# Fewer, larger logits batches, one more FP32 sum on VectorE, and down sums run ahead, in an attention + GLU kernel

## The chip, the cores and the metric

The kernel runs on one core of one Trainium2 chip. The metric is device microseconds of one execution. The granted TensorE clock was 1.000 in profiled runs. TensorE is called PE below, its weight loads PEld, VectorE DVE, ScalarE ACT.

## The reference, cut to what matters

```python
# x: [1, 2048, 640]; H = 32 heads of Dh = 20; window of W = 8 keys, 2 apart
xn = layernorm(x)
q, k, v = split(xn @ wqkv)                            # per head
logits[s, w] = q[s] . k[s - 2 w] / sqrt(Dh)           # -1e9 where s - 2w < 0
attn = softmax(logits over w)
o[s] = sum_w attn[s, w] * v[s - 2 w]
out = x + o @ wo + ((xn @ w_gate) * (xn @ w_up)) @ w_down     # F = 1536
```

## The kernel before

This kernel doesn't compute attention as matrix products of q and k on PE. DVE makes the elementwise products, and PE adds them up by multiplying with small 0/1 matrices in its 32-column tiling mode (four 128x32 tiles side by side). All other work of PE (projections, gate and up, down and output) uses the whole 128x128 array and serves as filler. PE's sums go to PSUM, a memory that the program divides into eight banks of 512 columns; "ACT evicts" means that ACT copies a bank out, after which it can be used again. A planner written in Python decides, while the program is built, where each visit to the 32-column mode goes in PE's fixed instruction order; it does so with a running estimate of PE's and DVE's time (`t_pe`, `t_dve`).

The 40 products of q and k go through a ring of buffers and are added up in batches:

```python
def qk_logits(batch):                                  # batch: list of (w, c, slot)
    for w, c, s in batch:
        for j in range(NJ):                            # four 32-column tiles, one per 512 tokens
            ... matmul(PS[32*j:32*j+32, lb], G[:, c, :], prd(s)[:, j*JB:(j+1)*JB],
                       start=(c == 0), stop=(c == NCH-1), tile_position=(0, 32*j))
    ... ACT evicts the logits of every w that is now complete

for i, (w, c) in enumerate(order):                     # 40 products
    t_dve[0] = ... + 1.14
    qk_prod(w, c, i % NPW)                             # DVE, ring of NPW = 11
    batch.append((w, c, i % NPW))
    if ready is not None and len(batch) == 2:
        run_fill(ready[1])                             # PE filler up to the time estimated
        qk_logits(ready[0]); ready = None
    if i % 20 in (7, 15, 19):                          # batches of 8, 8, 4, 8, 8, 4
        ready = (batch, t_dve[0] + 0.2); batch = []
```

The value side has 20 units (4 token blocks of 512 x 5 channel groups). A "plain" unit is one DVE pass, whose two halves PE adds up with eight matmuls. Any other unit is three DVE passes: two products in FP32 and their sum. PE then needs four matmuls.

```python
PLAIN = {0: PA, 1: PB, 2: PC, 3: PV, 4: PC, 19: PA}
GROUPS = ((0, 1, 2), (3, 4), tuple(range(5, 10)), tuple(range(10, 15)), tuple(range(15, 20)))
# pv_sum(us): PE sums of one group, one PSUM bank per unit, then ACT evicts each into OT

def tail(t, nb):                                       # output, 128 tokens x 320 columns
    b = bank()
    for i in range(NF + NCH):                          # 12 down matmuls, then 5 of the output projection
        l, x = (HT[...], WD[:, i, cols]) if i < NF else (OT[...], WO[:, i - NF, cols])
        ... matmul(PS[:, b], l, x, start=(i == 0), stop=(i == n - 1))
    ... DVE adds the residual; store
```

## Time and profile before

Three runs gave a median of 272.38 us (271.96 to 272.39). The span of the profiled run is 270.3 us.

| what | before |
|---|---|
| PE busy | 266.5 us, 99% |
| DVE busy | 224.5 us, 83% |
| ACT busy | 117.1 us, 43% |
| PE's share of the chain that ended last | 93% |

The first two lines are from the profile's page. Each engine has its busy us, share of the span and number of instructions.

```profile
span 270.3 us, 4471 instructions
PE 266.5 (99%) x1837; PEld 149.4 (55%) x1837; DVE 224.5 (83%) x276; ACT 117.1 (43%) x213; POOL 2.5 (1%) x18
```

"PE busy" alone is weak evidence. The Trainium skill, "Perfetto Trace Analysis", section "Tensor Engine Instruction (MATMUL, LD_WEIGHTS)", says that the profiler estimates the end of a matmul. This trace fits that, without proving it: a 128x512 matmul is given as 379 ns, yet the next starts about 216 ns after it (95 of them take 20.50 us below), so the durations given overlap. What ends last is told better by the chain, the work followed back from the last instruction. Its columns are start us, duration us, what (in the first line L443, projections of 256 columns). L424 are projections, L473 logits, L588 the sums of the value side, L648 down and output matmuls.

```profile
19.61 10.92 PE PS L443 x100
30.53 20.50 PE PS L424 x95
51.03 1.84 PE PS L473 x32
52.87 7.66 PE PS L424 x35
60.53 1.84 PE PS L473 x32
62.37 2.26 PE PS L424 x10
64.64 0.98 PE PS L473 x16
...
73.28 1.84 PE PS L473 x32
...
82.78 1.84 PE PS L473 x32
...
86.88 0.98 PE PS L473 x16
...
238.63 1.41 PE PS L588 x24
240.04 27.87 PE PS L648 x221
267.91 0.02 issue
```

Each line of the chain starts where the one before it ends (lines left out are marked by dots): from 15.25 us on, the chain is PE without a break. A wait shorter than the overlap, 379 - 216 = 163 ns, would not show as a break, so the starts of the single matmuls count too (in the packed trace each has its own record): after 19.61 us, two 128x512 matmuls in the 128x128 mode start 0.215 to 0.227 us apart and two 128x320 ones 0.135 to 0.147 us; longer steps (0.229 to 0.312 us) come at changes of the tiling mode alone. So PE doesn't wait, and the lengths of the lines tell what a visit to the 32-column mode costs. 32 logits matmuls take 1.84 us and 16 take 0.98 us, so four take (1.84 - 0.98) / 4 = 0.215 us and a visit has 0.12 us on top of its work. The projections behind it (35 in 7.66 us) are also 0.1 us longer than at PE's pace.

### The profile page before, as it was taken

The page shows a single profiled execution, that of the slowest core. Times are in us where ns is not written, and L with a number is a line of the kernel's source. Part 1 is how long each engine was busy: PE and PEld are TensorE (multiplying, and loading weights), DVE is VectorE, ACT ScalarE, POOL GpSimd, SP SyncE. Part 2 cuts the span into 40 slices and gives each one's busy share as a digit, 9 for nine tenths or more (in the row PEclk, how much of TensorE's full clock was granted, in tenths as well). Part 3 has the DMA queues.
Part 4 walks back from the last instruction along what each step waited for, and adds up shares of the span by engine and source line. Part 5 has one row for each costly group of instructions (what it writes and reads, how often), then busy time and mean ns, then how long its engine had stood idle before and what let it go on. Part 6 is the DMA issues. An engine that isn't in the chain of part 4 may idle for free.

```text
span 270.3 us, 4471 instructions
## 1 busy us (share of the span) xinstructions
PE 266.5 (99%) x1837; PEld 149.4 (55%) x1837; DVE 224.5 (83%) x276; ACT 117.1 (43%) x213; POOL 2.5 (1%) x18
## 2 busy tenths in 40 slices
PE   8999999999999999999999999999999999999996
PEld 3998644444443444444467744446764444767775
DVE  5899719999996799899998999999999999922212
ACT  3665666355555684666530037551007555030000
POOL 2000000000000000000000000000000000000000
DMA  6998699018989597679324341232421000021301
GB/s 205 316 134 152 103 300 402 25 57 343 387 346 406 178 358 263 182 173 338 125 82 127 94 147 66 78 81 79 142 84 49 0 2 0 27 72 49 96 29 49
DMA packets 35668, 41.53 MB, mean 154 GB/s; under 512 B 10304, under 2 KB 31808, under 8 KB 35648
## 3 DMA queue, kind: packets, MB, share of 16 engines
q1 hardware_dynamic: 35344, 40.96, 49.0%
q10 hardware_dynamic: 304, 0.30, 0.4%
q8 instruction: 14, 0.23, 0.3%
q14 instruction: 6, 0.05, 0.1%
HBM read 25.07 MB, written 13.16 MB: 141 GB/s over the span
## 4 chain that ended last, share of the span: by engine, by line
PE 93%; SPq 2%; DMA 1%; DVE 1%; issue 0%; ACT 0%
PE PS L617 39%; PE PS L648 27%; PE PS L424 16%; PE PS L443 4%; PE PS L473 3%; PE PS L588 2%; SPq L288 2%; PE PS L436 2%; DMA XST<-in_A_x_dram 1%; DVE XNS L378 0%; DVE STATS L356 0%; DVE STATS L362 0%; DVE MV L368 0%; DVE FOUT L652 0%; ACT SD L369 0%
## 5 line engine op out<-in xcount | busy, mean ns | idle before, releaser
L617 PE MATMUL PS<-XNT,WG 128*128 128x512 bf16 x240 | 59.7, 379 | 0.0
L617 PE MATMUL PS<-XNT,WU 128*128 128x512 bf16 x240 | 59.6, 379 | 0.0
L648 PE MATMUL PS<-WD,HT 128*128 128x320 bf16 (+1 forms) x396 | 57.6, 295 | 0.0
L619 ACT ACTIVATE HT<-PS 128x512 bf16<-128x512 f32 x48 | 28.8, 599 | 58.8 <-PE PS L617 57.0
L648 PEld LDWEIGHTS PS<-WD,HT 128*128 128x128 bf16 x396 | 38.1, 98 | 15.0 <-issue 0.4
L424 PE MATMUL PS<-XNT,WQKV 128*128 128x512 bf16 x200 | 44.0, 379 | 0.0
L617 PEld LDWEIGHTS PS<-XNT,WU 128*128 128x128 bf16 x240 | 23.4, 98 | 28.5 <-issue 0.4
L617 PEld LDWEIGHTS PS<-XNT,WG 128*128 128x128 bf16 x240 | 23.1, 98 | 28.9 <-ACT OT L594 0.8
L619 ACT ACTIVATE USX<-PS 128x512 bf16<-128x512 f32 x48 | 28.8, 600 | 20.1 <-PE PS L617 20.1
L652 DVE TENSOR_TENSOR FOUT<-PS,XR 128x320 bf16<-128x320 f32 (+1 forms) x33 | 15.7, 477 | 25.6 <-PE PS L648 25.5
L465 DVE TENSOR_TENSOR PRA<-QT,KT 128x2048 bf16<-128x2048 bf16 x24 | 27.6, 1218 | 7.3 <-ACT KT L429 7.3
L424 PEld LDWEIGHTS PS<-XNT,WQKV 128*128 128x128 bf16 x200 | 19.2, 98 | 24.2 <-issue 1.3
L565 DVE TENSOR_TENSOR TB<-VX,ATX 128x2048 f32<-128x2048 bf16 x14 | 31.9, 2282 | 0.0
L565 DVE TENSOR_TENSOR TA<-VX,ATX 128x2048 f32<-128x2048 bf16 x14 | 31.9, 2282 | 0.0
L648 PE MATMUL PS<-WO,OT 128*128 128x320 bf16 (+1 forms) x165 | 27.1, 295 | 0.0
L648 PEld LDWEIGHTS PS<-WO,OT 128*128 128x128 bf16 x165 | 15.9, 98 | 5.9
L622 DVE TENSOR_TENSOR HT<-HT,USX 128x512 bf16<-128x512 bf16 x48 | 19.0, 416 | 0.0
L465 DVE TENSOR_TENSOR PRB<-QT,KT 128x2048 bf16<-128x2048 bf16 x16 | 18.5, 1218 | 0.0
L429 ACT ACTIVATE VST<-PS 128x512 bf16<-128x512 f32 x20 | 12.0, 599 | 11.6 <-PE PS L424 11.6
L594 ACT ACTIVATE OT<-PS 128x512 bf16<-128x512 f32 x20 | 10.3, 609 | 9.0 <-PE PS L588 9.0
L574 DVE TENSOR_TENSOR SV<-TA,TB 128x2048 bf16<-128x2048 f32 x6 | 13.7, 2283 | 0.0
L436 PE MATMUL PS<-XNT,WQKV 128*128 128x128 bf16 x200 | 12.3, 219 | 0.4 <-ACT KT L451 0.3
(72 smaller groups left out, 190.4 us busy)
## 6 DMA issues: line engine op xcount, KB each, us to landing
VX<-v_scratch SPq DMA_DIRECT2D x20, 520.0 KB, 4.8
v_scratch<-VST SPq DMA_DIRECT2D x5, 515.5 KB, 6.5
v_scratch<-VST SPq DMA_DIRECT2D x5, 515.0 KB, 6.2
v_scratch<-VST SPq DMA_DIRECT2D x5, 514.5 KB, 5.3
v_scratch<-VST SPq DMA_DIRECT2D x5, 514.0 KB, 4.2
XR<-in_A_x_dram SPq DMA_DIRECT2D x16, 160.0 KB, 2.5
XST<-in_A_x_dram SPq DMA_DIRECT2D x15, 160.0 KB, 4.0
out_dram<-FOUT SPq DMA_DIRECT2D x15, 160.0 KB, 1.8
```

Of the source, the lines that this page charges most:

```text
L424: op("pe", (lambda l, x, c: lambda e: e.matmul(PS[:, b, :], l, x, start=(c == 0), stop=(c == NCH - 1)))(l, x, c), r=[l, x], w=[PS[:, b, :] ...
L429: op("act", lambda e: e.activation(o, PS[:, b, :], ACT.Copy), r=[PS[:, b, :]], w=[o], name=f"pev{which}_{m}_{j}")
L436: op("pe", (lambda o, l, x, st, sp: lambda e: e.matmul(o, l, x, start=st, stop=sp))(o, l, x, st, sp), r=[l, x], w=[o], name=f"pp{which}_{m ...
L443: op("pe", (lambda l, x, c: lambda e: e.matmul(o, l, x, start=(c == 0), stop=(c == NCH - 1)))(l, x, c), r=[l, x], w=[o], name=f"pw{which}_ ...
L465: op("dve", lambda e: e.tensor_tensor(prd(s), QT[:, c, :], k, ALU.mult), r=[QT[:, c, :], k], w=[prd(s)], name=f"prod{w}_{c}")
L565: op("dve", lambda e: e.tensor_tensor(t[:], vw, a, ALU.mult), r=[v, at[:, r, :], ("tsum", 0)], w=[t[:]], name=f"pv{u}_{r}")
L574: op("dve", lambda e: e.tensor_tensor(s[:], TA[:], TB[:], ALU.add), r=[TA[:], TB[:]], w=[s[:], ("tsum", 0)], name=f"pa{u}")
L617: op("pe", (lambda l, x, c: lambda e: e.matmul(PS[:, b, :], l, x, start=(c == 0), stop=(c == NCH - 1)))(l, x, c), r=[l, x], w=[PS[:, b, :] ...
L619: op("act", lambda e: e.activation(o, PS[:, b, :], ACT.Copy), r=[PS[:, b, :]], w=[o], name=f"guev{which}_{m}_{j}")
L622: h_pending.append(lambda: op("dve", lambda e: e.tensor_tensor(h, h, o, ALU.mult), r=[h, o], w=[h], name=f"h{m}_{j}"))
L648: op("pe", (lambda l, x, i, b: lambda e: e.matmul(PS[:, b, 0:wid], l, x, start=(i == 0), stop=(i == n - 1)))(l, x, i, b), r=[l, x], w=[PS[ ...
L652: op("dve", (lambda o, xr, b: lambda e: e.tensor_tensor(o, PS[:, b, 0:wid], xr, ALU.add))(o, xr, b), r=[PS[:, b, :], xr], w=[o], name=f"fi ...
```

## The change

Its intent: fill the 32-column mode better (10 products a visit, 4 visits for 6), with a larger ring so that DVE needn't wait; let DVE do the final sum of unit 19 too; and start the last token block's output groups with their down matmuls, which don't need attention, in three banks that stay open. One softmax maximum is split, so that most of it can run before the last logit. The core of the diff, with cuts marked:

```diff
-    NPA, NPW = 6, 11
+    NPA, NPB, NPW = 6, 5, 13
+    PRC = sb("PRC", [128, S], at=a_ra + 20 * JB * 2)          # and PRE: two more ring slots
...
-    PLAIN = {0: PA, 1: PB, 2: PC, 3: PV, 4: PC, 19: PA}
+    PLAIN = {0: PA, 1: PB, 2: PC, 3: PV, 4: PC}
...
-                (0.67, tt(M1, L[:, 0:4], L[:, 4:8], ALU.max, "smax1")),
+                (0.4, tt(M1[:, 3:4], L[:, 3:4], L[:, 7:8], ALU.max, "smax1")),
+            early = (0.55, tt(M1[:, 0:3], L[:, 0:3], L[:, 4:7], ALU.max, "smax0"))
...
-    def tail(t, nb):
+    def tail(t, nb, span=(0, NF + NCH)):
-            b = bank()
+            b = held_banks.pop((t, nb)) if span[0] else bank()
-            for i in range(n):
+            for i in range(*span):
+            if span[1] < n:
+                held_banks[t, nb] = b
+                return
...
-    LATE = 1.2
+    LATE = (1.2, 1.2, 2.5, 2.5, 1.2)
-    add_dn(3)
+    add_dn(3, 3)            # first the down matmuls of three groups, later their output matmuls
...
-        if i % 20 in (7, 15, 19):
-            ready = (batch, t_dve[0] + 0.2)
+        if i % 20 in (9, 19):
+            ready = (batch, t_dve[0] - 0.6)
```

`LATE` is how long after DVE's estimated end the planner puts a group's sums into PE's order.

More of the change, by code (lines that the diff above doesn't have):

```diff
@@ L232, in build_kernel @@
     a_pr = place[0]
-    NPA, NPW = 6, 11
+    NPA, NPB, NPW = 6, 5, 13
     PRA = sb("PRA", [128, NPA, S])
-    PRB = sb("PRB", [128, NPW - NPA, S], at=a_wd)
+    PRB = sb("PRB", [128, NPB, S], at=a_wd)
+    PRC = sb("PRC", [128, S], at=a_ra + 20 * JB * 2)
     def prd(s):
-        return PRA[:, s, :] if s < NPA else PRB[:, s - NPA, :]
+        if s < NPA + NPB:
+            return PRA[:, s, :] if s < NPA else PRB[:, s - NPA, :]
+        return PRC[:] if s == NPA + NPB else PRE[:]
     a_pc = a_qk + 8 * 4 * VW * 2
@@ L279, in build_kernel @@
     G = sb("G", [128, NCH, H])
+    PRE = sb("PRE", [128, S])
     PS = nc.alloc_psum_tensor("PS", [128, 8, 512], FP32)
@@ L518, in half @@
             ]
-            return head, rest
-        (h0, r0), (h1, r1) = half(0), half(1)
-        return h0 + h1 + r0 + r1
+            early = (0.55, tt(M1[:, 0:3], L[:, 0:3], L[:, 4:7], ALU.max, "smax0"))
+            return early, head, rest
+        (e0, h0, r0), (e1, h1, r1) = half(0), half(1)
+        return [e0, e1] + h0 + h1 + r0 + r1
     def attn_move(j):
@@ L630, in build_kernel @@
     stores = []
-    def tail(t, nb):
+    held_banks = {}
+    def tail(t, nb, span=(0, NF + NCH)):
         j, rows = t // 4, slice((t % 4) * TS, (t % 4 + 1) * TS)
@@ L767, in build_kernel, with add_dn @@
     units_done = [0]
-    def add_dn(j):
-        for st in range(4):
-            for nb in range(2):
-                fill.append(("dn", j, lambda st=st, nb=nb: tail(4 * j + st, nb)))
+    def add_dn(j, ahead=0):
+        groups = [(4 * j + st, nb) for st in range(4) for nb in range(2)]
+        for t, nb in groups[:ahead]:
+            fill.append((1.63, lambda t=t, nb=nb: tail(t, nb, (0, NF))))
+        for i, (t, nb) in enumerate(groups):
+            span = (NF if i < ahead else 0, NF + NCH)
+            fill.append(("dn", j, 0.136 * (span[1] - span[0]), lambda t=t, nb=nb, span=span: tail(t, nb, span)))
     add_gu(0)
@@ L789, in run_fill @@
                     return
-                t_pe[0] += 2.31
+                t_pe[0] += it[2]
                 t_dve[0] += 0.41
-                it[2]()
+                it[3]()
             else:
@@ L822, in build_kernel @@
     qk_logits(ready[0])
-    t_pe[0] = max(t_pe[0], ready[1]) + 1.13
+    t_pe[0] = max(t_pe[0], ready[1]) + 0.21 + 0.22 * len(ready[0])
     t_dve[0] = max(t_dve[0], t_pe[0] + 1.0)
@@ L857, in buf_name @@
         return t.name.split("_")[0]
-    for us in GROUPS:
+    for us, late in zip(GROUPS, LATE):
         for u in us:
@@ L870, in build_kernel @@
             take()
-        pend.append((us, t_dve[0] + LATE))
+        pend.append((us, t_dve[0] + late))
     take()
```

## The prediction

> **What bounds the kernel now.** TensorE's instruction stream. The page gives PE 99% busy, 266.5 of 270.3 us at clock 1.000; DVE 83%, ACT 43%. In the chain of waits PE is 93%, and from 15.25 us to the last result at 267.91 us it is PE without a break. The list of waits shows, after 15 us, only gaps of 0.4 us in the weight-load row, at changes between 128-column and 32-column matmuls. DVE's idle time (28 us of it in the last 30 us) is free. So the change can save only what it takes out of TensorE's stream, and lose only by making that stream wait.
>
> **What leaves TensorE.** (1) Logits go in 4 batches (10 products each) instead of 6 (8, 8, 4 twice). In the chain 32 logits matmuls last 1.84 us and 16 last 0.98 us: 0.215 us per four plus 0.12 us per batch; the projection stretch after a batch is longer too (35 matmuls 7.66 us, against 35 x 0.2155 = 7.54). A visit costs about 0.23 us beyond its work; two fewer save 0.46 us. The Trainium skill, "TensorEngine Tiling (Array Packing)", Key Properties, says that changing the tiling mode drains TensorE; this trace agrees, with those 0.23 us. (2) Unit 19 is summed in FP32 on DVE, so TensorE adds up one half of products, not two: four 32-column matmuls fewer, 0.22 us. Together 0.68 us, all on the critical path. The down sums run ahead are only reordered: same matmuls, same tiling mode, 0.
>
> **What is moved or added, off the chain.** Unit 19 costs DVE three passes of 2.28 us instead of one: +4.6 us. The split of the first softmax maximum saves 0.4 us per half, but the last logits batch is bigger and later: I put it at 88.3 to 90.6 us (86.8 to 87.8 before), so attention starts some 2 us later on DVE. The ring of 13 leaves DVE three products (1.14 us each) while PE adds up a batch of 2.3 us, and each batch starts 1 to 3 us after its last product, so neither should stall there.
>
> Does PE then wait for DVE at the sums? By the changed order, with durations of the trace: first sums at PE about 122.0 us (118.1 before), their products ready about 119.4; groups three and four about 167.9 and 207.1, ready about 164.3 and 204.4; the last about 247.4 (238.6 before), because all eight output groups of the third token block now precede it, and unit 19's sum is ready about 246. Margins 1.4 to 4 us. The last ScalarE evictions (five, 2.56 us) hide behind the 36 down matmuls run ahead (4.9 us). With five banks for sums and three held, the eight suffice.
>
> **Predicted time:** 272.38 - 0.68 = 271.7 us; 8 times in 10 within 270.9 to 272.7. Faster by over 2%: 0.01. Within 2%: 0.97. Slower by over 2%: 0.02.
>
> **What would show it.** In the chain, four logits stretches of about 2.27 us (9.1 us in all, 9.3 before). Still no PE wait on DVE beyond the 0.4 us gaps. The last sums start near 247 us, then 36 down and 15 output matmuls in one stretch. DVE busy grows by about 4.6 us to 229 us; PE busy falls by less than 1 us. The tail from the last sums to the end shortens from 29 to about 20 us, with no gain in the span.
>
> **What would make it wrong.** DVE falling over 1.4 us behind my placing at unit 19, so that PE waits before its last sums; a product ring that stalls DVE at slot reuse; the shorter tail leaving ScalarE, banks or the residual loads too little time (a wait in the last 20 us); a mode change that costs more or less than 0.23 us.

## The result, and the profile after

The changed kernel took 271.50 us (median of 6 runs, 271.08 to 271.67) against 272.03 us of the kernel before in the same rounds (6 runs, 271.89 to 272.39). The ratio is 0.9976, with a 95% interval of 0.9963 to 0.9988. Ratios here are the mean time of one kernel's runs over that of the other's of the same rounds, so not quite the ratio of the medians quoted. The change is a gain of a quarter of a per cent, about 0.65 us.

The same two lines of the page, after:

```profile
span 269.7 us, 4451 instructions
PE 263.8 (98%) x1817; PEld 149.2 (55%) x1833; DVE 228.6 (85%) x280; ACT 117.2 (43%) x213; POOL 2.5 (1%) x18
```

DVE has 4.1 us more to do, as unit 19's FP32 sum asks. PE's 2.7 us less can't be taken at its word: the program has 1833 matmuls, of which each loaded its weights, and only 1817 are in this trace. The chain shows the lost records as gaps of 0.05 or 0.16 us called "issue" and as stretches of 49 for 50; where one is lost between two 128x512 matmuls, they start 0.432 us apart, twice 0.216, so nothing waited there. From the x100 line on, PE is busy 246.26 us here, and 247.63 us in the trace of no_ahead (below), which has the same matmuls and all records: the lost ones account for 1.4 us of the 2.7, a different start (before the x100 line) for 0.6, and the change for the rest. The chain after (L428 projections, L477 logits, L593 sums, L655 down and output):

```profile
19.67 10.92 PE PS L447 x100
...
52.17 2.27 PE PS L477 x40
...
65.34 1.65 PE PS L477 x28
...
76.35 2.27 PE PS L477 x40
...
88.44 2.27 PE PS L477 x40
...
122.12 1.41 PE PS L593 x24
...
247.49 1.19 PE PS L593 x20
248.68 18.64 PE PS L655 x153
267.31 0.02 issue
```

There are four visits for the logits where there were six. Three are given with 2.27 us. The one at 65.34 us is cut short to 28 matmuls only because the chain leaves PE for ACT there: the record of the projection behind it is lost. All its 40 matmuls are in the trace, and the next projection recorded is 2.43 us on (67.77 us), as after the visit at 52.17 us (2.27 us and an "issue" of 0.16). The last sums have 20 matmuls where they had 24. The last sums come 8.9 us later than before and the end comes 0.6 us earlier. So the shorter tail is nearly all a move.

In this tail, the timeline (start us, duration us, engine, line, operation, out<-in, shape, count) shows why nobody waits:

```profile
243.60 2.28 DVE L579 TENSOR_TENSOR SC<-TA,TB 128x2048 bf16<-128x2048 f32 x1
247.42 0.40 PE L593 MATMUL PS<-SD,SEL 128*32 128x512 bf16 x4
247.87 2.56 ACT L599 ACTIVATE OT<-PS 128x512 bf16<-128x512 f32 x5 [18.22 <-PE PS L593]
248.61 5.06 PE L655 MATMUL PS<-WD,HT 128*128 128x320 bf16 x36
253.51 2.20 PE L655 MATMUL PS<-WO,OT 128*128 128x320 bf16 x15
```

Unit 19's sum is written at 245.88 us, 1.5 us before PE turns to the sums and some 2.4 us before PE reaches unit 19 in them. ACT's five evictions end at 250.43 us, 3 us before their first reader at 253.51 us.

### A ruler finer than the timing

Times of one kernel scatter by 0.25 to 0.9 us (those of late2 by 1.7), as much as the effect. Part of that is the start: the first stretch of 100 projection matmuls (128x256) begins between 19.56 and 20.23 us in the traces. In the latest of them (no_ahead) the load of x at the head of the chain took 4.62 us, against 4.01 us in the kernel before. From there to PE's last matmul the chain is PE alone, and that stretch is called the PE stretch below: start plus duration of the chain's last PE line, less the start of the x100 line. Before it is 240.04 + 27.87 - 19.61 = 248.30 us, after it is 248.68 + 18.64 - 19.67 = 247.65 us. The difference, 0.65 us, agrees with the timed ratio (0.24% of 272 us). The stretch is read from one trace of each kernel.

### The profile page after: what moved, and what is told of

Its sections match the earlier page's. It is cut to its first block, busy times and chain, and to the rows that moved or that the text cites. A ratio compares the mean times of both kernels' runs of the same rounds, so it can differ in the third digit from the quotient of the medians.

```text
span 269.7 us, 4451 instructions
## 1 busy us (share of the span) xinstructions
PE 263.8 (98%) x1817; PEld 149.2 (55%) x1833; DVE 228.6 (85%) x280; ACT 117.2 (43%) x213; POOL 2.5 (1%) x18
## 4 chain that ended last, share of the span: by engine, by line
PE 93%; SPq 2%; DMA 2%; DVE 1%; issue 1%; ACT 1%
PE PS L622 38%; PE PS L655 27%; PE PS L428 16%; PE PS L447 4%; PE PS L477 3%; PE PS L593 2%; SPq L292 2%; PE PS L440 2%; DMA XST<-in_A_x_dram 2%; DVE XNS L382 0%; DVE STATS L360 0%; DVE STATS L366 0%; ACT LOG L484 0%; DVE MV L372 0%; DVE FOUT L662 0%
## 5 line engine op out<-in xcount | busy, mean ns | idle before, releaser
L622 PE MATMUL PS<-XNT,WU 128*128 128x512 bf16 x237 | 59.0, 379 | 0.3 <-issue 0.2
L622 PE MATMUL PS<-XNT,WG 128*128 128x512 bf16 x232 | 57.9, 379 | 0.5 <-issue 0.2
L655 PE MATMUL PS<-WD,HT 128*128 128x320 bf16 (+1 forms) x396 | 57.3, 295 | 0.0
L655 PEld LDWEIGHTS PS<-WD,HT 128*128 128x128 bf16 x396 | 38.1, 98 | 15.0 <-issue 0.4
L428 PE MATMUL PS<-XNT,WQKV 128*128 128x512 bf16 x195 | 42.9, 379 | 0.6 <-issue 0.3
L570 DVE TENSOR_TENSOR TA<-VX,ATX 128x2048 f32<-128x2048 bf16 x15 | 34.3, 2286 | 0.1
L570 DVE TENSOR_TENSOR TB<-VX,ATX 128x2048 f32<-128x2048 bf16 x15 | 34.3, 2284 | 0.0
L428 PEld LDWEIGHTS PS<-XNT,WQKV 128*128 128x128 bf16 x200 | 19.3, 98 | 23.9 <-issue 0.8
L469 DVE TENSOR_TENSOR PRA<-QT,KT 128x2048 bf16<-128x2048 bf16 x19 | 21.9, 1221 | 7.3 <-ACT KT L433 7.3
L655 PE MATMUL PS<-WO,OT 128*128 128x320 bf16 (+1 forms) x165 | 26.8, 295 | 0.0
L655 PEld LDWEIGHTS PS<-WO,OT 128*128 128x128 bf16 x165 | 15.9, 98 | 5.9
L469 DVE TENSOR_TENSOR PRB<-QT,KT 128x2048 bf16<-128x2048 bf16 x15 | 17.3, 1222 | 0.0
L579 DVE TENSOR_TENSOR SC<-TA,TB 128x2048 bf16<-128x2048 f32 x6 | 13.7, 2283 | 0.0
```

Source lines behind the costliest of these rows:

```text
L428: op("pe", (lambda l, x, c: lambda e: e.matmul(PS[:, b, :], l, x, start=(c == 0), stop=(c == NCH - 1)))(l, x, c), r=[l, x], w=[PS[:, b, :] ...
L469: op("dve", lambda e: e.tensor_tensor(prd(s), QT[:, c, :], k, ALU.mult), r=[QT[:, c, :], k], w=[prd(s)], name=f"prod{w}_{c}")
L570: op("dve", lambda e: e.tensor_tensor(t[:], vw, a, ALU.mult), r=[v, at[:, r, :], ("tsum", 0)], w=[t[:]], name=f"pv{u}_{r}")
L579: op("dve", lambda e: e.tensor_tensor(s[:], TA[:], TB[:], ALU.add), r=[TA[:], TB[:]], w=[s[:], ("tsum", 0)], name=f"pa{u}")
L622: op("pe", (lambda l, x, c: lambda e: e.matmul(PS[:, b, :], l, x, start=(c == 0), stop=(c == NCH - 1)))(l, x, c), r=[l, x], w=[PS[:, b, :] ...
L655: op("pe", (lambda l, x, i, b: lambda e: e.matmul(PS[:, b, 0:wid], l, x, start=(i == 0), stop=(i == n - 1)))(l, x, i, b), r=[l, x], w=[PS[ ...
```

## The experiments

Theory: PE's stream decides. A visit to the 32-column mode costs a fixed 0.2 us, a group of four 32-column matmuls 0.215 us, and all else in the change costs or gains nothing. Rivals: DVE's extra work is paid for or its relief gains; the larger ring or the down sums run ahead are what gains.

| kernel | ratio to before, 95% interval | median us | PE stretch us | less before |
|---|---|---|---|---|
| before | | | 248.30 | |
| changed | 0.9976 (0.9963 to 0.9988) | 271.50 | 247.65 | -0.65 |
| batches_only | 0.9985 (0.9973 to 0.9998) | 271.71 | 247.85 | -0.45 |
| unit19_only | 0.9985 (0.9972 to 0.9999) | 271.79 | 248.08 | -0.22 |
| no_ahead | 0.9981 (0.9967 to 0.9994) | 271.50 | 247.65 | -0.65 |
| batch5 | 1.0013 (0.9998 to 1.0028) | 272.54 | 248.63 | +0.33 |
| batch2 | 1.0103 (1.0088 to 1.0119) | 274.84 | 251.17 | +2.87 |
| ring11 | 0.9972 (0.9958 to 0.9986) | 271.36 | 247.65 | -0.65 |
| plain3 | 1.0053 (1.0039 to 1.0066) | 273.49 | 249.72 | +1.42 |
| plain3_later | 1.0006 (0.9990 to 1.0023) | 272.21 | 248.29 | -0.01 |
| late1 | 0.9983 (0.9968 to 0.9998) | 271.52 | 247.65 | -0.65 |
| late2 | 1.0080 (1.0055 to 1.0105) | 274.03 | 249.96 | +1.66 |
| late2_ahead | 0.9976 (0.9959 to 0.9993) | 271.36 | 247.65 | -0.65 |
| best_merge | 0.9968 (0.9956 to 0.9981) | 271.24 | 247.42 | -0.88 |

The twelve experiments gave correct results. All diffs below are against the changed kernel. The larger ring (but for ring11), the split maximum and the later `LATE` of two groups stay in all of them; the last two were not tried alone. The sums below leave nothing over for them.

### The parts of the change, one at a time

**batches_only**: the batches of 10 without the other two parts.

```diff
-    PLAIN = {0: PA, 1: PB, 2: PC, 3: PV, 4: PC}
+    PLAIN = {0: PA, 1: PB, 2: PC, 3: PV, 4: PC, 19: PA}
-    add_dn(3, 3)
+    add_dn(3)
```

> The change without unit 19's FP32 sum and without the down sums run ahead; the ring of 13 and the batches of 10 stay. Theory (the stream of TensorE decides, and each visit to the 32-column mode costs about 0.23 us beyond its work): two visits fewer, 0.46 us less than before, ratio 0.9983; four logits stretches of 2.27 us in the chain. Rival (the gain comes from DVE no longer being held by the ring or from an earlier softmax): softmax starts some 2 us later here, so the time would be equal or longer, ratio 1.000 or more.

Measured: ratio 0.9985, PE stretch 0.45 us shorter. As the theory had it, although softmax starts later.

**unit19_only**: the FP32 sum of unit 19 without the other two.

```diff
-        if i % 20 in (9, 19):
-            ready = (batch, t_dve[0] - 0.6)
+        if i % 20 in (7, 15, 19):
+            ready = (batch, t_dve[0] + 0.2)
-    add_dn(3, 3)
+    add_dn(3)
```

> The change without the batches of 10 (logits in 8, 8, 4 twice as before, the ring of 13 stays and is not filled) and without the down sums run ahead; unit 19 is summed in FP32. Theory: four 32-column matmuls fewer and nothing else, 0.22 us less than before, ratio 0.9992, DVE busy 4.6 us longer. Rival (DVE's extra 4.6 us are paid for): ratio above 1.003.

Measured: PE stretch 0.22 us shorter, with DVE 4.2 us busier (228.7 us). The timed ratio, 0.9985, is lower than expected, but its interval (0.9972 to 0.9999) takes in 0.9992. So DVE's 4.2 us are free, and the rival's 1.003 is excluded. By the PE stretch 0.45 + 0.22 = 0.67, against 0.65 for the whole change: the parts add up.

**no_ahead**: no down sums run ahead.

```diff
-    add_dn(3, 3)
+    add_dn(3)
```

> The change without the down sums run ahead. Theory: one group's 12 down matmuls (1.6 us) after the last sums already cover the five ScalarE evictions up to where each is needed, so the time is that of the changed kernel, 0.66 us less than before, ratio 0.9976. Rival (the down sums run ahead hide a wait): a TensorE wait of 0.5 to 2 us after the last sums, ratio 0.9995 to 1.005.

Measured: PE stretch 247.65 us, that of the changed kernel. The timed ratio of 0.9981 doesn't differ from it either. Here, the down sums run ahead gain nothing.

### What a visit costs

**batch5** and **batch2** add up the same 40 products in 8 and in 20 visits.

```diff
-        if i % 20 in (9, 19):
-            ready = (batch, t_dve[0] - 0.6)
+        if i % 5 == 4:                       # batch2: i % 2 == 1
+            ready = (batch, t_dve[0] + 0.2)
```

> The changed kernel with logits in 8 batches of 5 products. Theory: 4 visits more than the changed kernel, 0.92 us; against before 2 visits more and four matmuls fewer, +0.24 us, ratio 1.001. Rival (visits are free): 0.998. With the batches of 2 and of 10 this should lie on one line of 0.23 us a visit.

> The changed kernel with logits added up in 20 batches of 2 products. Theory: 16 visits to the 32-column mode more than the changed kernel, at 0.23 us each 3.7 us; against before 14 visits more and four matmuls fewer, +3.0 us, ratio 1.011. Rival (the gain of the change came from the ring, visits are free): ratio 0.998.

Measured, with 4, 8 and 20 visits: PE stretch 247.65, 248.63 and 251.17 us. From 4 to 20 that is 3.52 / 16 = 0.22 us a visit. The 8 visits lie 0.1 us above that line; their first took 1.30 us where the other seven took 1.19: by the timeline PE stopped after 12 of its 20 matmuls, until ACT had emptied a PSUM bank of its projection at 48.62 us (PE goes on at 48.67). In the chain of the 20 visits, both halves of the cost can be read:

```profile
43.44 0.55 PE PS L477 x8
43.99 2.27 PE PS L428 x10
46.25 0.55 PE PS L477 x8
...
50.80 0.55 PE PS L477 x8
51.34 3.34 PE PS L428 x15
```

8 logits matmuls take 0.55 us, of which 2 x 0.215 is work and 0.12 the way in. 10 projections take 2.27 us, of which 10 x 0.2155 is work and 0.11 the way out. The starts of the single matmuls, which no estimated end enters, give much the same: 0.31 us from the last projection to the first logits matmul, and 0.31 us from the last logits matmul to the next projection, where one step is else 0.21 to 0.22. A change of work within the 128x128 mode costs nothing: from the last gate or up matmul to the first down matmul it is 0.216 us, as between two of the former.

The Trainium skill, "TensorEngine Tiling (Array Packing)", section "Key Properties", says that a change of the tiling mode drains TensorE. These runs fit that, and give a figure: 0.22 us for both changes of a visit. What PE does in that time they don't show.

### Is the larger ring needed?

**ring11**: 11 slots as before, but batches of 10, emitted one product earlier.

```diff
-    NPA, NPB, NPW = 6, 5, 13
+    NPA, NPB, NPW = 6, 5, 11
-        if ready is not None and len(batch) == 2:
+        if ready is not None and len(batch) == 1:
```

> The changed kernel with a ring of 11 as before, batches of 10, the logits emitted after one more product and not two. Theory: DVE stalls some 2 us once, near 64 us, for the slot of the second batch's first product, but TensorE takes the last batch some 3 us after the last product, so the time is the changed kernel's, ratio 0.9976 (within 0.001). Rival (the larger ring is what makes the larger batch possible): TensorE waits or softmax comes too late, +1 us or more against the changed kernel, ratio above 1.001.

Measured: PE stretch 247.65 us again, ratio 0.9972. DVE does stall, where it was expected (line of the timeline, the bracket is the idle time before):

```profile
65.84 1.23 DVE L469 TENSOR_TENSOR PRB<-QT,KT 128x2048 bf16<-128x2048 bf16 x1 [1.72 <-PE PS L477]
```

The stall of 1.72 us costs nothing. What gained is the size of the batch; the two further slots only spare DVE a stall that costs no time.

### Does DVE's work count?

**plain3**: units 9, 14 and 19 as plain units: 12.4 us less for DVE by the page (216.2 us), 12 matmuls more for PE.

```diff
-    PLAIN = {0: PA, 1: PB, 2: PC, 3: PV, 4: PC}
+    PLAIN = {0: PA, 1: PB, 2: PC, 3: PV, 4: PC, 9: PA, 14: PA, 19: PA}
```

> The changed kernel with units 9, 14 and 19 left unsummed by DVE. Theory: DVE has 13.7 us less to do (about 215 us busy) and TensorE 12 matmuls more (four of them as in the kernel before), 0.65 us longer than the changed kernel, ratio 1.000 against before. Rival (DVE, 85% busy, also bounds the kernel): faster than the changed kernel, ratio 0.995 or less.

Measured: a miss. PE stretch 249.72 us, 2.07 us above the changed kernel, where 0.65 was expected. The rival (faster with a relieved DVE) is refuted, but 1.4 us are left over. The timeline of the last sums shows them:

```profile
229.63 2.28 DVE L560 TENSOR_TENSOR PA<-VX,ATX 128x4096 bf16<-128x4096 bf16 x1
230.41 0.39 PE L593 MATMUL PS<-SC,SEL 128*32 128x512 bf16 x4
232.06 0.61 PE L593 MATMUL PS<-PA,SEL 128*32 128x512 bf16 x8 [1.25 <-ACT OT L599]
```

PE stands in the middle of the sums (the bracket counts from an estimated end; by the starts, the step is 1.63 us where 0.21 is usual, 1.42 us too long). The profile names as the releaser ACT's eviction of another unit of these sums, which ended 0.02 us after DVE's product. But the matmuls read PA, which DVE finishes at 231.91 us, 0.15 us before PE goes on, and the PSUM bank that they write was last used four groups of gate and up matmuls earlier. In plain3_later (next), the same eight matmuls start at 234.82 us, before the first eviction of these sums ends at 234.99 us, so they need none of them. The planner had put these sums too early for DVE's last product.

**plain3_later**: the same, with two output groups put before these sums.

```diff
+    PLAIN = {0: PA, 1: PB, 2: PC, 3: PV, 4: PC, 9: PA, 14: PA, 19: PA}
-    LATE = (1.2, 1.2, 2.5, 2.5, 1.2)
+    LATE = (1.2, 1.2, 2.5, 2.5, 4.0)
```

> The run with units 9, 14 and 19 unsummed came out 2.0 us above the changed kernel, not 0.65; its trace shows TensorE waiting 1.3 us within the last sums, until 0.2 us after unit 19's product is written. Here two output groups of the third token block go before those sums, otherwise the same. Theory (TensorE came too early for DVE's last product, a fault of the order and not a cost of DVE having less to do): the wait goes and the time is 0.65 us above the changed kernel, ratio 1.000 against before (0.9985 to 1.0015). Rival (unsummed units cost TensorE more than their four extra matmuls each, by banks or ScalarE): ratio stays at 1.005.

Measured: ratio 1.0006, PE stretch 248.29 us, 0.64 us above the changed kernel: 12 matmuls at 0.215 us per four. The wait is gone with the order alone changed, so it was a fault of the order. A kernel with 12 us less work for DVE is slower by exactly what PE has more.

### How much slack DVE has, and what the down sums run ahead are good for

**late1** and **late2** repeat unit 19's last DVE pass once and twice, with PE's order untouched. **late2_ahead** repeats it twice and puts two of the three groups of down matmuls before the last sums.

```diff
                   name=f"pa{u}")
+            if u == 19:
+                for _ in range(2):                       # late1: range(1)
+                    op("dve", ...the same TA + TB into s..., name="again")
# late2_ahead also:
-    LATE = (1.2, 1.2, 2.5, 2.5, 1.2)
+    LATE = (1.2, 1.2, 2.5, 2.5, 5.0)
```

> The changed kernel with unit 19's last DVE pass done twice, so that its sum is ready 2.2 us later, near 248.1 us; TensorE needs it near 248.3 us. Theory (DVE has about 2.4 us of slack at the last sums): no change against the changed kernel, ratio 0.9976 (within 0.001). Rival (DVE's work is paid for in the span): +2.2 us, ratio 1.006.

> The same with that pass done three times: the sum is ready near 250.3 us, TensorE needs it near 248.3 us. Theory: a TensorE wait of about 2 us in the last sums and +2 us against the changed kernel, ratio 1.005. Rival (there is slack of more than 4.4 us): ratio 0.9976.

> As the run before (that pass three times), but with two of the three groups of down sums run ahead put in front of the last sums, the third behind them. Theory: the down sums in front move TensorE's need by 3.2 us to about 251.5 us, the wait goes away and the time is the changed kernel's, ratio 0.9976 (within 0.001): what the down sums run ahead are worth is slack for DVE, which the changed kernel doesn't use. Rival (the sums then come too late for the ScalarE evictions): a wait of 1 to 2 us before the output matmuls, ratio 1.002 or more.

Measured: one repetition is free (PE stretch 247.65 us), with little to spare: the sum is written at 248.27 us and PE takes it in a stretch that begins at 248.13 us, with unit 18's four matmuls first (so unit 19's turn comes at about 248.35 us). The second costs 2.31 us in the PE stretch (2.5 us by the medians, with runs from 273.47 to 275.17, the longest at a clock of 0.994). The ratio, 1.0080, lies above the 1.005 expected, and its interval excludes it. This is a small miss: the two passes take 4.62 us where 4.4 were reckoned, and the four runs scatter by 1.7 us; more isn't known. In the timeline of late2 PE waits for the sum (again the bracket counts from an estimated end and is some 0.16 us short):

```profile
246.39 4.62 DVE L583 TENSOR_TENSOR SC<-TA,TB 128x2048 bf16<-128x2048 f32 x2
248.54 0.39 PE L597 MATMUL PS<-SC,SEL 128*32 128x512 bf16 x4
251.06 0.40 PE L597 MATMUL PS<-SC,SEL 128*32 128x512 bf16 x4 [2.13 <-DVE SC L583]
```

In late2_ahead, the same DVE work is free again:

```profile
245.88 4.62 DVE L583 TENSOR_TENSOR SC<-TA,TB 128x2048 bf16<-128x2048 f32 x2
247.28 3.42 PE L659 MATMUL PS<-WD,HT 128*128 128x320 bf16 x24
250.64 0.40 PE L597 MATMUL PS<-SD,SEL 128*32 128x512 bf16 x4
251.83 1.80 PE L659 MATMUL PS<-WD,HT 128*128 128x320 bf16 x12
```

PE fills the time with 24 down matmuls, and its stretch is 247.65 us. So the down sums run ahead can be made into slack: about 3.3 us of it (24 x 0.136) when two groups are put before the last sums. The changed kernel puts them after the sums and needs none of it.

### A version that beats both

**best_merge**: the changed kernel, with the first two groups of sums made one; unit 4's product goes where the logits lay.

```diff
+    PL = sb("PL", [128, 4, 2, JB], at=a_log)
-    PLAIN = {0: PA, 1: PB, 2: PC, 3: PV, 4: PC}
+    PLAIN = {0: PA, 1: PB, 2: PC, 3: PV, 4: PL}
-    GROUPS = ((0, 1, 2), (3, 4), tuple(range(5, 10)), ...
+    GROUPS = (tuple(range(5)), tuple(range(5, 10)), ...
-    LATE = (1.2, 1.2, 2.5, 2.5, 1.2)
+    LATE = (2.5, 2.5, 2.5, 2.5)
# HOLDS, the planner's list of which buffers overlap, gets "PL": {6, 7}
```

> The change, with the first two groups of sums (units 0 to 2 and 3 to 4) added up in one visit of TensorE; unit 4's products lie where the logits were. Theory: one more visit to the 32-column mode saved, 0.23 us below the changed kernel, 0.89 us below before, ratio 0.9967. Rival (visits cost nothing by themselves): ratio as the changed kernel's, 0.9976. The two differ by about the width of the interval, so the chain (one sums stretch of about 2.27 us in place of 1.41 and 0.98 us with two gaps after them) is to tell.

Measured: ratio 0.9968, median 271.24 us, PE stretch 247.42 us: 0.23 us below the changed kernel. The chain has one stretch of 40 in place of two:

```profile
90.60 37.88 PE PS L623 x175
128.48 2.27 PE PS L594 x40
```

It beats the kernel before. That it also beats the changed kernel is shown by the PE stretch, not by the timing alone (the intervals overlap).

## Why the prediction was right

- **What bounds the kernel.** Right. Adding a DVE pass (late1), taking 12 us off DVE (plain3_later) and stalling DVE (ring11) left the PE stretch as PE's own work has it.
- **What leaves PE.** 0.46 us for two visits: 0.45 measured. 0.22 us for four matmuls: 0.22 measured. Together 0.68 us predicted, 0.65 us in the PE stretch and in the timed ratio. The time itself was put at 271.7 us and came out at 271.50: most of these 0.2 us are the starting point, 272.38 us, which was the median of three runs of the kernel before, where all six of the comparison gave 272.03. The range given (270.9 to 272.7 us) also takes in the kernel before, so it is the chain and the experiments that bear the prediction out, not the time alone. The cost of a visit was put at 0.23 us; the series of batches gives 0.22.
- **The down sums run ahead, 0.** Right (no_ahead). That they would not be used as slack was read from the changed order: they come after the last sums.
- **What is moved on DVE.** Right in direction, off in size. Attention starts 3.0 us later on DVE (first product at 112.50 us, before 109.51), where 2 us were predicted. So the margins at the sums were overestimated for three groups: the first sums' products were ready at 120.54 us (predicted 119.4), group three's at 166.56 (164.3), group four's at 206.13 (204.4). PE turned to them, by the chain, at 122.12, 168.01 and 207.21 us (predicted 122.0, 167.9, 207.1). The margins there were 1.1 to 1.6 us, predicted 2.6 to 3.6. The last was right: ready at 245.88 (246), PE at 247.42 (247.4). None became a wait, so the time didn't show this error. That none did is in part luck: the products came 1.1 to 2.3 us later than I had placed them, and 1.1 us was left at group four.
- **Why PE's times were met to 0.1 us, DVE's were not.** PE has no waits in this stretch, so its times follow from counting matmuls. DVE's contain waits for others (1.55 us for a DMA just before the first product at 112.50 us, where it was 1.23 before), which I only carried over from the profile of before. How the 3.0 us are made up in full was not worked out.

The miss was in an experiment, not in the prediction: plain3 was expected to cost 0.65 us and cost 2.07, because I checked the matmul counts of the new order and not whether DVE would be ready for it.

## What to carry to other kernels

Where the chain is one engine without a break, price a change by what it adds to and takes from that engine's own instruction stream, then check that nothing new makes it wait; work that only other engines gain or lose is worth nothing until a margin turns negative. In these kernels a visit to the other tiling mode cost 0.22 us on top of its work, with batches of 2 products as of 10, so the larger batches gained and the larger ring didn't. To resolve a change of a few tenths of a per cent, measure a stretch of the trace that excludes the noisy start: five of these kernels agreed on 247.65 us within 0.01, and most others differed from it by a countable number of matmuls and visits, while the single times of these five lay between 271.08 and 272.06 us.

## What the Trainium skill lacked or had wrong

- "TensorEngine Tiling (Array Packing)", Key Properties: says that a change of tiling mode drains TensorE, but gives no cost. Here it was 0.22 us for a visit from the 128x128 mode to four 128x32 tiles and back, about half of it on the way in and half on the way out (20 against 4 visits: 3.52 us more).
- "TensorE: Matmul & The Clock Gate", section "Measured speedup vs the span model", gives 2.38 times for three column tiles with N=512. No page has a measured figure for four of them, one set behind the other. In the middle of a visit four 128x32 matmuls of N=512 took 0.215 us, the time of one 128x128 matmul of N=512 (10 in 2.16 us): four tiles at the price of one, once the visit's fixed cost is set apart. As the tile counts differ, this doesn't show the page's figure wrong.
- "Perfetto Trace Analysis", section "Tensor Engine Instruction (MATMUL, LD_WEIGHTS)", says that the end of a matmul is estimated, but not that a wait can hide in the overlap: at 379 ns given and 216 ns apart, PE counts as busy through a wait of up to 163 ns. The page doesn't say either that matmul records can be missing: 16 of the changed kernel's 1833 were, and from the x100 line on it shows 246.26 us of PE busy time, where no_ahead, with the same matmuls and all records, shows 247.63.
